# Transposing the first half batch from its float32 load tiles, moving the third to the DMA crossbar, and splitting the last output tile

## The chip, the cores and the metric

The kernel runs on one core of one Trainium2 chip. The metric is device time in microseconds (us) of one execution. Engines are called as the profile calls them: PE is the matrix engine, PEld its weight loads, DVE the vector engine, ACT the scalar engine, POOL the general engine, SP the engine that issues the DMA transfers.

## The reference

Sliding-window attention with four sink tokens feeds a gated feed-forward network:

```python
scores = scale * np.matmul(q, k.transpose(0, 1, 3, 2))          # B 4, H 8, S 768, D 64
keep = is_sink | in_window                                      # 4 sinks, window of 128
a = softmax(where(keep, scores, -1e9))
x = matmul(a, v).transpose(0, 2, 1, 3).reshape(3072, 512)
h = x @ w_in                                                    # 512 x 2048
g = h * (1.0 / (1.0 + np.exp(-beta * h)))
out = g @ w_out                                                 # 2048 x 512, float32
```

All inputs and the output are float32. Both kernels compute in bfloat16 after a cast.

## The kernel before

The work is cut into eight "half batches" of 384 tokens. Each has four units, a unit being a pair of heads. For a unit the kernel transposes q and k, computes scores, masks and exponentiates them, and multiplies by v. Then come the input projection (384-column matmuls) and the output projection (512-column matmuls) of the half batch. PE does all matmuls, so PE is the engine to keep busy.

The file is a small planner: it creates every instruction with a guess of its duration in ns, places the instructions on the engines by those guesses, and writes them out. From then on every engine has its own list, in a fixed order.

The half batches get their transposed q and k in one of two ways. `XB` says how many take the first way; the others take the second:

```python
# first way: cast to bf16, then six PE transposes per unit into one PSUM bank, one copy to SBUF
def T(u):
    ...
    for i, n in enumerate("qk"):
        for c in range(NK):
            add("pe", lambda e, i=i, n=n, c=c: nc.tensor.transpose(
                mp[:, i * HALF + c * 128:i * HALF + (c + 1) * 128],
                x16[n][hb % NX][:, c, 2 * hp:2 * hp + 2, :].rearrange("p h d -> p (h d)"), ident[:, :]),
                mm_ns(128), r=[(n + "16", hb % NX, hp, c), "ident"], x=[("B", bs[0])])
    any_of(copies(unitT(u).rearrange("p a (s j) -> p a s j", j=NK),
                  mp[:, 0:2 * HALF].rearrange("p (a j s) -> p a s j", a=2, j=NK), {"dve": 868, "act": 690}),
           w=qkey(u), x=[("B", bs[0])])

# second way: cast to bf16, then the DMA transposes q (or k) of the whole half batch
def XT(hb, i):
    ...
    add("sp", lambda e: e.dma_start_transpose(...), ...)
```

The window masks of the scores are `affine_select` instructions on POOL; the masks of the sinks may be on POOL or DVE. The output transposes of the first `XB` half batches are PE transposes as well; the later ones go through the crossbar. `mix` is the order in which early attention loads (`a`) and weight loads (`w`) are issued.

The softmax here doesn't subtract the row's maximum and nothing guards it: scores larger than these inputs give would overflow.

Of the kernel before, what the change touches and what calls it, by code (L numbers as in the profile page):

```python
# [22 lines left out]
PAR = {'AHEAD': 300,  # L23
 'BACKLOG': 3000,
 'KEEP': 300,
 'KEPT': 0,
 'MARGIN': 800,
 'M_AV': 200,
 'M_H': 0,
 'M_O': 0,  # L30
 'M_OT': 0,
 'M_SC': 1000,
 'M_SS': 2000,
 'M_T': 500,
 'XB': 3,
 'mix': 'wawawawwwawawwawwaaawwwawawaaaaa',
 'prio': ('SC', 'SS', 'OT', 'AV', 'T')}
# [7 lines left out]
class Graph:  # L45
# [8 lines left out]
    SLACK = 0  # L54
    LEAD = 1500
    COLD, WARM = 217, 150
# [68 lines left out]
    def place(self, o, at):  # L125
        o.at = at
        if o.dma:
# [11 lines left out]
            o.end = self.dma_free + 950  # L139
# [20 lines left out]
    def arrange(self):  # L160
# [37 lines left out]
        while todo_pe or pool:  # L198
# [14 lines left out]
            for o in pool:  # L213
                opts = []
                for e, (fn, ns) in o.alts.items():
                    t = max(self.free[e], ready(o, e))
                    if o.dma:
                        t = max(t, self.dma_free - self.LEAD)
                    opts.append((t + ns, t, e))
                _, t, e = min(opts)  # L220
                by_eng.setdefault(e, []).append((t, o))
# [161 lines left out]
def _program(nc, G, sb, ps, q, k, v, w_in, w_out, beta, out):  # L383
    NU = 2 * NPAIR
    NSTG, NX, NV, NT, NE, NON, NG, NTT, NOS, NKS, NWS = 2, 2, 3, 8, 4, 4, 3, 3, 3, 4, 6
    XB, PB = PAR.get('XB', 3), 2
    NK = NB // 2
    ident = sb("ident", (128, 128), BF16)
    ones = sb("ones", (128, 128), BF16)
    maskS = sb("maskS", (128, 2, 128), BF16)  # L390
# [32 lines left out]
    def unitT(u):  # L423
        return qkT_all[:, u // 4 % (NT // 4), :, :].rearrange("p a (h t) -> p a h t", h=4)[:, :, u % 4, :]

    def tokens(u, i, rows, t0, n):
        hb = u // 4
        if hb < XB:
            return unitT(u)[rows, i, t0:t0 + 128 * n].rearrange("p (s w) -> p s w", w=128)
        t = qkT_all[rows, hb % (NT // 4), i, :].rearrange("p (c h w) -> p c h w", h=4, w=128)  # L430
        return t[:, t0 // 128:t0 // 128 + n, u % 4, :]

    def qkey(u):
        return [("qkT", u % NT, i, c) for i in range(2) for c in range(NK)]

    def any_of(alts, r=(), w=(), x=()):

        return G.add(min(alts, key=lambda e: G.free[e] + alts[e][1]), None, 0, r, w, x, None, alts)
# [17 lines left out]
    def where(u):  # L456

        return u // 8, u // 4 % 2, u % 4
# [4 lines left out]
    def choose(n):  # L463

        if n == 4:
# [36 lines left out]
    def consts():  # L502
# [5 lines left out]
        for i, sg in ((0, -1), (1, 1)):  # L508
            add("gp", lambda e, i=i, sg=sg: e.affine_select(
                headm[:, i:i + 1], ones[:, 0:1], [[0, 1]], ALU.is_ge, 0.0, base=63 if i == 0 else -64,  # L510
                channel_multiplier=sg), 110, r=["ones"], w=["headm"] if i else ["headm0"])
        for i in range(NV):
# [12 lines left out]

        add("act", lambda e: e.activation(warm[:, :], ones[0:1, 0:1], AF.Exp, bias=0.0, scale=1.0), 1300,
# [17 lines left out]
    def load(hb, n, i):  # L544

        b, t0, z = hb // 2, hb % 2 * HALF, hb % NSTG
        if n != "v" and XB <= hb < XB + NSTG:
# [8 lines left out]
        elif hb >= XB:  # L556
# [30 lines left out]
    def cast(hb, n, i):  # L587
# [5 lines left out]
        elif hb < PB:  # L593
# [4 lines left out]
        elif hb >= XB:  # L598
# [5 lines left out]
        if hb < PB and n != "v":  # L604
# [13 lines left out]
    def T(u):  # L618

        G.begin()  # L620
        hb, hp = u // 4, u % 4
        bs = take(1)
        mp = P[:, bs[0], :].bitcast(BF16)
        for i, n in enumerate("qk"):
            for c in range(NK):
# [4 lines left out]
        any_of(copies(unitT(u).rearrange("p a (s j) -> p a s j", j=NK),  # L630
                      mp[:, 0:2 * HALF].rearrange("p (a j s) -> p a s j", a=2, j=NK), {"dve": 868, "act": 690}),
               w=qkey(u), x=[("B", bs[0])])
        sinks(u)
        give(bs)

    def sinks(u):
        hb, hp = u // 4, u % 4
        if hb % 2 == 0:
            ks = u % NKS
            kd = kS[ks][:, :].rearrange("p (a w) -> p a w", w=32)[:, 0:2, 0:NSINK]  # L640
            add("gp", lambda e: e.tensor_tensor(
                kd, tokens(u, 1, slice(0, 128), 0, 1)[:, :, 0:NSINK].to_broadcast([128, 2, NSINK]),
                headm[:, :].unsqueeze(2).to_broadcast([128, 2, NSINK]), ALU.mult), 200,
                r=[("kS", ks), ("qkT", u % NT, 1, 0), "headm0", "headm"], w=[("kSd", ks)])

    def XT(hb, i):
        n, s0 = "qk"[i], 4 * hb % NT
# [6 lines left out]
            w=[("qkT", s0 + j, i, c_) for j in range(4) for c_ in cs], dma=f"dx{n}{hb % 2}", queue=1540, ring=999, lag=1350)  # L654
# [7 lines left out]
    def slots(half):  # L662

        out_, i = {}, 0
        for j, grp in enumerate(GROUPS[half]):
# [5 lines left out]
    def SC(u):  # L671
        G.begin()
        b, half, hp = where(u)
        z = u % NE
        bs = take(4)
        for j, grp in enumerate(GROUPS[half]):

            jobs = {}
            for i, (kind, kb, qb) in enumerate(grp):
                jobs.setdefault(kb, []).append((qb, i))  # L680
            for kb, cols in jobs.items():
                cols.sort()
                own = u if kb >= NK * half else u - 4
# [3 lines left out]
                for hh in range(2):  # L687
# [4 lines left out]
                        dst, tokens(own, 1, rows, kc, 1)[:, 0, :], tokens(u, 0, rows, q0, nq),  # L692
                        start=True, stop=True), mm_ns(128 * nq) / 2 + 24,
                        r=qkey(u) + qkey(own), x=[("B", bs[2 * j + hh])])
        for j, grp in enumerate(GROUPS[half]):
            n, s0 = len(grp), slots(half)[grp[0]][1]
# [4 lines left out]
            for kind, sg in (("d", 1), ("p", -1)):  # L701
                at_ = [i for i, blk in enumerate(grp) if blk[0] == kind]
                if at_:
                    d = E[z][:, s0 + at_[0]:s0 + at_[-1] + 1, :, :].rearrange("p s h w -> p (s h) w")
                    add("gp", lambda e, d=d, sg=sg, at_=at_: e.affine_select(  # L705
                        d, d, [[0, 2 * len(at_)], [sg, 128]], ALU.is_ge, 0.0, base=min(sg, 0), channel_multiplier=-sg),
                        pool_ns(256 * len(at_), 2 * len(at_)), r=[("E", z, j)], w=[(kind, z, j)])
# [7 lines left out]
    def SS(u):  # L715

        G.begin()
        b, half, hp = where(u)
        z, ks = u % NE, (u - 4 * half) % NKS
        q0 = 0 if half else 256  # L720
        bs = take(1)
        add("pe", lambda e: e.matmul(  # L722
            P[:, bs[0], q0:HALF].rearrange("p (s w) -> p s w", w=128), kS[ks][:, :],
            tokens(u, 0, slice(0, 128), q0, (HALF - q0) // 128), start=True, stop=True), mm_ns(HALF - q0),
            r=[("kSd", ks)] + qkey(u), x=[("B", bs[0])])
        add("act", lambda e: e.activation(ES[z][:, q0:HALF], P[:, bs[0], q0:HALF], AF.Exp, bias=0.0, scale=SCALE),  # L726
            act_ns(HALF - q0), w=[("ES", z)], x=[("B", bs[0])])
        give(bs)

    def parts(half):  # L730

        sl = slots(half)
        return [[(blk[0], sl[blk][0], sl[blk][1], blk[1])
                 for blk in sorted(sl, key=lambda x: "spd".index(x[0])) if blk[2] == qb]
                for qb in range(NK * half, NK * half + NK)]

    def av_keys(u):
        z = u % NE
        ks = {(p[0], z, p[1]) for ps in parts(where(u)[1]) for p in ps}
        return sorted(ks) + [("v", u // 4 % NV, c) for c in range(NK)] + [("ES", z), ("vSd", u // 8 % 2, 1)]  # L740

    def AV(u):
        G.begin()
        b, half, hp = where(u)
        z, on = u % NE, u % NON
        bs = take(1)
        A = P[:, bs[0], :]
        for m, ps in enumerate(parts(half)):
            far = NK * half + m >= 2
            if far:  # L750
                c0 = 2 * m * (D + 1)
                add("pe", lambda e, m=m, c0=c0: e.matmul(  # L752
                    A[:, c0:c0 + 2 * (D + 1)], ES[z][:, m * 128:(m + 1) * 128],
# [3 lines left out]
            for hh in range(2):  # L757
                c0 = (2 * m + hh) * (D + 1)
                for n, (kind, j, i, kb) in enumerate(ps):
                    vz = (u if kb >= NK * half else u - 4) // 4 % NV  # L760
                    add("pe", lambda e, c0=c0, hh=hh, i=i, kb=kb, vz=vz, a=(n == 0 and not far), o=(n == len(ps) - 1):
                        e.matmul(A[:, c0:c0 + D + 1], E[z][:, i, hh, :], vaug[vz][:, kb % NK, 2 * hp + hh, :],  # L762
                                 start=a, stop=o, skip_group_check=True), 39,
                        r=[(kind, z, j), ("v", vz, kb % NK)], x=[("B", bs[0])])
        av = A[:, 0:2 * NK * (D + 1)].rearrange("p (a e) -> p a e", e=D + 1)
        add("dve", lambda e: e.reciprocal(rden[on][:, :].unsqueeze(2), av[:, :, D:D + 1]), 105,  # L766
# [326 lines left out]
```

## Time and profile before

| | before |
|---|---|
| median (range) of its runs | 230.72 us (230.68 to 231.6) |
| span of the profiled run | 228.6 us |
| PE busy | 96% |
| granted PE clock | 1.00 from the first record of it, at 6.1 us, to the last matmul |
| first input-projection matmul | 17.22 us |
| last v load issued | 143.0 us |

Two lines of the page give the busy time of each engine, in us, share of the span and instructions. After them comes the row of DMA busy tenths, with the span in 40 equal slices, then the line of the DMA queue that carries nearly everything (packets, MB, share of 16 engines' time), and the shares of the chain of work that ended last.

```profile
span 228.6 us, 4534 instructions
PE 218.7 (96%) x1756; PEld 121.5 (53%) x1756; DVE 137.1 (60%) x295; ACT 154.0 (67%) x276; POOL 72.6 (32%) x161
...
DMA  6999999999999999999999999621120311011112
...
q1 hardware_dynamic: 94112, 39.47, 75.8%
...
PE 79%; DVE 7%; DMA 7%; SPq 4%; ACT 2%; issue 1%; POOL 0%; POOLq 0%
```

PE is the limit, and 79% of the chain lies on it.

The timeline shows where the start ends and where the tail begins, as start, us, engine, line, operation, and in brackets the idle time before and what ended it. The waits view gives the only long wait of a projection, in us, times and longest.

```profile
17.22 1.73 PE L805 MATMUL P<-xT,w_in 128*128 128x384 bf16 x8
...
225.30 0.60 ACT L492 ACTIVATE osb<-P 128x512 f32<-128x512 f32 x1 [2.86 <-PE P L825]
```

```profile
PE P L805 <- DVE w_in L497: 2.0, 2, 1.1
```

### The profile page before, as it was taken

The numbers are of one execution on the slowest core, as the hardware profiler recorded it, in microseconds if no ns is written. First come the engines' busy times: TensorE is split into PE (matmuls) and PEld (weight loads), VectorE is DVE, ScalarE is ACT, GpSimd is POOL, SyncE is SP. The second block draws the span as 40 slices with busy tenths as digits, with TensorE's granted clock in tenths as the row PEclk, the third lists the DMA queues.
The fourth block names the chain that finished last, engine by engine and source line by source line (L and its number), as shares of the span: only waits on it lengthen the run. The fifth ranks groups of instructions, "written<-read, shape, count | busy, mean of one in ns | idle before, by whom it ended". The sixth has DMA issues, their size and how long they took to land.

```text
span 228.6 us, 4534 instructions
## 1 busy us (share of the span) xinstructions
PE 218.7 (96%) x1756; PEld 121.5 (53%) x1756; DVE 137.1 (60%) x295; ACT 154.0 (67%) x276; POOL 72.6 (32%) x161
## 2 busy tenths in 40 slices
PE   8987899989999999899999999999999999999994
PEld 5653454646555556455554554655556555555541
DVE  3697888467966787565766773655346433633310
ACT  2986897469867796676885847768778454744431
POOL 6590047523244861152241733204544000000000
PEclk9999999999999999999999999999999999999999
DMA  6999999999999999999999999621120311011112
GB/s 175 241 333 380 373 373 244 307 266 241 237 182 249 227 110 210 238 199 238 222 199 218 238 191 195 170 80 46 37 67 16 80 46 46 4 46 46 46 49 92
DMA packets 94133, 39.76 MB, mean 174 GB/s; under 512 B 80784, under 2 KB 86944, under 8 KB 94112
## 3 DMA queue, kind: packets, MB, share of 16 engines
q1 hardware_dynamic: 94112, 39.47, 75.8%
q8 instruction: 14, 0.23, 0.4%
q14 instruction: 7, 0.06, 0.1%
HBM read 27.27 MB, written 6.29 MB: 147 GB/s over the span
## 4 chain that ended last, share of the span: by engine, by line
PE 79%; DVE 7%; DMA 7%; SPq 4%; ACT 2%; issue 1%; POOL 0%; POOLq 0%
PE P L825 33%; PE P L805 30%; PE P L691 5%; DMA q_stage<-in_q_dram 4%; PE P L762 3%; DMA k_stage<-in_k_dram 3%; PE P L1019 2%; SPq L564 2%; PE P L626 2%; DVE onorm L768 2%; DVE g L812 2%; PE P L722 1%; PE P L752 1%; PE P L781 1%; DVE w_in L497 1%; ACT t L810 1%
## 5 line engine op out<-in xcount | busy, mean ns | idle before, releaser
L805 PE MATMUL P<-xT,w_in 128*128 128x384 bf16 x512 | 97.3, 326 | 2.4 <-DVE w_in L497 2.0
L810 ACT ACTIVATE t<-P,hbeta 128x384 f32<-128x384 f32 x128 | 73.7, 584 | 37.5 <-PE P L805 33.2
L825 PE MATMUL P<-w_out,g 128*128 128x512 bf16 x384 | 96.3, 379 | 0.9 <-DVE g L812 0.8
L812 DVE SCALAR_TENSOR_TENSOR g<-t,P 128x384 bf16<-128x384 f32 x128 | 69.0, 550 | 45.2 <-ACT t L810 43.4
L705 POOL TENSOR_SCALAR_AFFINE_SELECT E<-E 128x512 bf16<-128x512 bf16 (+1 forms) x112 | 57.2, 542 | 71.5 <-ACT E L699 71.0
L805 PEld LDWEIGHTS P<-xT,w_in 128*128 128x128 bf16 x512 | 47.6, 98 | 39.5 <-DVE w_in L497 3.2
L825 PEld LDWEIGHTS P<-w_out,g 128*128 128x128 bf16 x384 | 35.8, 98 | 37.1 <-DVE g L812 3.2
L699 ACT ACTIVATE E<-P 128x768 bf16<-128x768 f32 x64 | 45.2, 759 | 9.3 <-PE P L691 9.3
L492 ACT ACTIVATE osb<-P 128x512 f32<-128x512 f32 x22 | 13.1, 597 | 11.5 <-PE P L825 11.3
L762 PE MATMUL P<-vaug,E 128*128 128x65 bf16 x352 | 18.4, 193 | 0.5 <-DVE vaug L497 0.5
L768 DVE TENSOR_TENSOR onorm<-P,rden 128x384 bf16<-128x384 f32 x32 | 17.8, 556 | 1.0
L762 PEld LDWEIGHTS P<-vaug,E 128*128 128x128 bf16 x352 | 16.2, 97 | 3.1 <-DVE vaug L497 0.6
L497 DVE CAST q<-q_stage 128x512 bf16<-128x512 f32 (+1 forms) x21 | 10.9, 521 | 8.7 <-DMA q_stage<-in_q_dram 8.7
L691 PE MATMUL P<-qkT 64*128 64x128 bf16 (+1 forms) x256 | 15.8, 239 | 0.1
L691 PEld LDWEIGHTS P<-qkT 64*128 64x128 bf16 x256 | 8.7, 94 | 11.5 <-issue 6.6
L726 ACT ACTIVATE ES<-P 128x128 bf16<-128x128 f32 (+1 forms) x32 | 11.5, 393 | 3.0 <-PE P L722 3.0
L752 PE MATMUL P<-vS,ES 128*128 128x130 bf16 x64 | 12.6, 220 | 0.0
L711 DVE TENSOR_TENSOR E<-E,maskS 128x512 bf16<-128x512 bf16 x16 | 7.8, 488 | 6.7 <-ACT E L699 6.7
L497 DVE CAST vaug<-v_stage 128x512 bf16<-128x512 f32 x15 | 7.4, 493 | 5.3 <-DMA v_stage<-in_v_dram 5.2
L492 ACT ACTIVATE qkT<-P 128x768 bf16<-128x768 bf16 x10 | 8.1, 820 | 3.7 <-PE P L626 3.7
L497 DVE CAST k<-k_stage 128x512 bf16<-128x512 f32 (+1 forms) x19 | 8.7, 459 | 2.9 <-DMA k_stage<-in_k_dram 2.7
L766 DVE RECIPROCAL rden<-P 128x6 f32<-128x6 f32 x32 | 6.1, 190 | 6.9 <-PE P L762 6.8
(48 smaller groups left out, 98.3 us busy)
## 6 DMA issues: line engine op xcount, KB each, us to landing
v_stage<-in_v_dram SPq DMA_DIRECT2D x24, 256.0 KB, 5.2
out_dram<-osb SPq DMA_DIRECT2D x24, 256.0 KB, 2.8
q_stage<-in_q_dram SPq DMA_DIRECT2D x15, 256.0 KB, 5.1
k_stage<-in_k_dram SPq DMA_DIRECT2D x15, 256.0 KB, 5.1
wst<-in_moe_w_in_dram SPq DMA_DIRECT2D x5, 512.0 KB, 7.4
wst<-in_moe_w_out_dram SPq DMA_DIRECT2D x4, 512.0 KB, 9.3
g<-in_moe_w_out_dram SPq DMA_DIRECT2D x4, 512.0 KB, 9.0
q_stage<-in_q_dram SPq DMA_DIRECT2D x8, 192.0 KB, 5.1
```

What stands on the lines that cost most here:

```text
L492: return lambda e: e.activation(dst, src, AF.Copy, bias=0.0, scale=scale)
L497: return lambda e: e.tensor_copy(dst, src)
L691: add("pe", lambda e, dst=dst, own=own, kc=kc, rows=rows, q0=q0, nq=nq: e.matmul(dst, tokens(own, 1, rows, kc, 1)[:, 0, :], tokens(u, 0, r ...
L699: add("act", lambda e, src=src, dst_=dst_: e.activation(dst_, src, AF.Exp, bias=0.0, scale=SCALE), act_ns(256 * n), w=[(k_, z, j) for k_ i ...
L705: add("gp", lambda e, d=d, sg=sg, at_=at_: e.affine_select(d, d, [[0, 2 * len(at_)], [sg, 128]], ALU.is_ge, 0.0, base=min(sg, 0), channel_ ...
L752: add("pe", lambda e, m=m, c0=c0: e.matmul(A[:, c0:c0 + 2 * (D + 1)], ES[z][:, m * 128:(m + 1) * 128], vS[b % 2][:, 2 * hp:2 * hp + 2, :]. ...
L762: e.matmul(A[:, c0:c0 + D + 1], E[z][:, i, hh, :], vaug[vz][:, kb % NK, 2 * hp + hh, :], start=a, stop=o, skip_group_check=True), 39,
L768: add("dve", lambda e: e.tensor_tensor(onorm[:, on, :, :], av[:, :, 0:D], rden[on][:, :].unsqueeze(2).to_broadcast([128, 2 * NK, D]), ALU. ...
L805: add("pe", lambda e, c=c: e.matmul(hp, w_in16[:, c, m * 128:(m + 1) * 128], xT[:, T_, c, :], start=(c == 0), stop=(c == 3)), mm_ns(HALF), ...
L810: add("act", lambda e: e.activation(tt[ti][:, :], hp, AF.Tanh, bias=0.0, scale=hbeta[:, m:m + 1]), act_ns(HALF) + 93, r=["hbeta"], w=[("t" ...
L812: add("dve", lambda e: e.scalar_tensor_tensor(gt[T_ % NG][:, m, :], tt[ti][:, :], 1.0, hp, ALU.add, ALU.mult), dve_ns(HALF), r=[("t", ti)] ...
L825: add("pe", lambda e, m=m: e.matmul(P[:, bk, :], gt[T_ % NG][:, m, t * 128:(t + 1) * 128], w_out16[:, m, :], start=(m == 0), stop=(m == NM ...
```

## The change

The intent is to shorten the start, to take PE work out of the saturated middle, and to shorten the tail:

- `RAW`: half batch 0 is transposed straight from its float32 load tiles, without the casts, by float32 matmuls against a float32 identity. Two of them occupy the two column halves of the array.
- `XB` 3 to 2: half batch 2 takes the crossbar, for q, k and the output transposes.
- `PB` 2 to 1 and a new `mix`: half batch 1 is loaded as two whole tensors and not as eight head pairs, and weights come earlier.
- `MD`: DVE may do the window masks, by a multiplication, where only POOL could.
- `CUT`: the last output tile is computed as 384 and 128 columns, each copied and stored by itself.
- New priorities and margins of the planner.

```diff
 PAR = {
-'AHEAD': 300, 'KEEP': 300, 'KEPT': 0, 'M_AV': 200, 'M_O': 0, 'M_OT': 0, 'M_SC': 1000,
+'AHEAD': 600, 'KEEP': 500, 'KEPT': -1, 'M_AV': 1000, 'M_O': 200, 'M_OT': 1000, 'M_SC': 0,
+'MD': 8, 'PB': 1, 'RAW': 1, 'l0': [7, 3, 0, 6, 2, 10, 5, 1, 4, 8, 9],
-'XB': 3,
-'mix': 'wawawawwwawawwawwaaawwwawawaaaaa',
-'prio': ('SC', 'SS', 'OT', 'AV', 'T')}
+'XB': 2,
+'mix': 'wwwawwwaaawaaawawwwwaaaawawwaawa',
+'prio': ('OT', 'AV', 'SS', 'SC', 'T')}
...
-    SLACK = 0
+    SLACK = 200
+    BIAS, EARLY = 150, 45000          # copies cost ACT 150 ns more in the plan before 45 us
...
+    def TR(hb, hp):
+        bs = take(2)
+        for i, n in enumerate("qk"):
+            for c in range(NK):
+                for hh in range(2):
+                    add("pe", lambda e, i=i, n=n, c=c, hh=hh: e.matmul(
+                        P[64 * hh:64 * hh + 64, bs[i], c * 128:(c + 1) * 128],
+                        stg[n][hb % NSTG][:, 2 * hp + hh, c, :], identF[:, :], start=True, stop=True,
+                        tile_position=(0, 64 * hh)), 116, ...)
+        for i in range(2):
+            any_of(copies(headT(hb, hp)[:, i, :].rearrange("p (s j) -> p j s", j=NK),
+                          P[:, bs[i], 0:HALF].rearrange("p (j s) -> p j s", j=NK), {"dve": 465, "act": 380}), ...)
...
+                    if UNITS[u][0] < PAR.get('MD', 2):
+                        alts["dve"] = (lambda e, d=d, mk=mk: e.tensor_tensor(d, d, mk, ALU.mult), ...)
...
+    cut = PAR.get('CUT', 384)
+    if cut:
+        OS[-4:] = [OS[-4 + j] + ab for ab in ((0, cut), (cut, NOUT)) for j in range(4)]
```

The rest of the long diff generalises the planner for half batches in parts.

## The prediction

It was written before anything of the change had been built or run.

> What bounds the kernel now. The busy table gives PE 96% of 228.6 us at clock 1.0, but that overlaps pipelined matmuls and includes fillers, so I count pitches from the timeline: 162 ns per 384-column input-projection matmul (512, 83 us), 216 ns per 512-column output-projection matmul (384, 83 us), 0.44 us per score unit, about 0.48 per value unit, 56 ns per 128-column transpose. Estimate: 205 us of PE work. The other 24 us lie, by the same count per window, in the start before the first input-projection matmul at 17.2 us (5.7 us of real work, 47 fillers, 11.5 lost), in 17.2 to 33 us (about 4 lost: the waits show PE waiting 2.0 us for w_in casts on DVE, whose loads are interleaved with half batch 1 while the DMA engines are full), about 3.4 in 46 to 140 us, and 3.4 of tail after the last matmul at 225.3. After 33 us PE is the limit.
>
> What the change does.
> 1. Half batch 0: eight casts (DVE 0.4 us each, the first 1.43) leave the start; 24 bf16 transposes become 48 float32 matmuls. The Trainium skill (FP8 and Floating Point Precision) says true FP32 takes 4 passes; TensorEngine Tiling says tiles operate independently. Estimate: 128 columns x 4 at 2.4 GHz is 213 ns, two at a time, so 1.3 us per unit against 0.34 to 0.44. No run here shows it yet. It fills time that fillers fill today. The 0.8 us PSUM copy becomes two of about 0.5 that ACT and DVE can share. First scores move from 6.6 us to about 5.9; first input projection to about 15.5 us: 1.5 us gained.
> 2. Weights are loaded earlier in the mix (six of the first seven loads after half batch 0, not four); half batch 1 comes in two large loads plus v. The stalls in 17 to 33 us should shrink: 2 us gained, with the risk that half batch 1 comes late.
> 3. Half batch 2 by crossbar: 24 q/k transposes and 12 output transposes leave PE, 36 x 56 ns = 2.0 us in the saturated stage, fully critical; their copies leave ACT/DVE. It adds two q/k transposes (3.9 to 4.2 us to landing) and two output ones (3.7 us) on a DMA share near 1. Some comes back as late loads: 1.5 us net.
> 4. DVE may mask score blocks in place of POOL everywhere, and priorities are retuned: 0 to 1 us, uncertain in sign.
> 5. Last tile in 384 and 128 columns: the last copy falls from 0.60 to about 0.3 us and its transfer to 64 KB, against about 0.2 us more PE: 0.4 us net.
>
> Sum: about 6 us. Predicted 224.9 us, 80% range 221.5 to 228.5. Faster by over 2%: 0.65; within 2%: 0.33; slower: 0.02.
>
> What would show it. Right: no q/k cast of half batch 0; the first input-projection matmul before 16.2 us; fewer fillers; PE waits for w_in casts under 1 us; 12 crossbar q/k and 12 output transposes in place of 10 and 10; last matmul to end of span under 3.1 us; last matmul near 219 to 222 us. Wrong: the four float32 units last over 10 us; first projection no earlier.
>
> What would make it wrong: column tiles that do not overlap; a drain at each change of tiling; crossbar transfers that delay loads so that PE waits in 46 to 140 us; half batch 1 scores late, leaving PE with no work between input and output projection; or the start being bound by DMA arrival alone, so that nothing starts earlier.

## More of the kernel before

For the second way, and for v always, a row of a transfer is 256 bytes; for the first way it is 768 bytes:

```python
def load(hb, n, i):
    ...
    if n == "v":
        src = v[b, :, t0 + i * 128:t0 + (i + 1) * 128, :].rearrange("h p d -> p h d")      # 256-byte rows
    elif hb >= XB:
        src = {"q": q, "k": k}[n][b, :, t0 + i * 128:t0 + (i + 1) * 128, :].rearrange("h p d -> p h d")
    else:
        hs = slice(0, H) if i is None else slice(2 * i, 2 * i + 2)
        src = {"q": q, "k": k}[n][b, hs, t0:t0 + HALF, :].rearrange("h (p j) d -> p h (j d)", j=NK)  # 768
```

The windows view gives, for a stretch of time, its length and the busy us of PE, PEld, DVE, ACT and POOL (with instructions), the granted clock as a share, the DMA share and GB/s.

```profile
27.00:36.00 9.00, 9.00 (x66) 4.71 (x65) 7.95 (x16) 8.94 (x17) 3.19 (x5) 1.00 1.06 373
...
141.00:160.00 19.00, 19.00 (x151) 10.51 (x150) 11.07 (x25) 14.48 (x29) 4.95 (x12) 1.00 0.41 105
```

In both stretches PE never rests, and by the second the loads are nearly over (last v load issued at 143.0 us, DMA share 0.41).

## The result

The change was built as given and is correct. Ratios here and below are the mean time of one kernel's runs over that of the other's of the same rounds, with a 95% interval, so they are not quite the ratio of the medians quoted. Executions over 1.5% slower than the fastest of the same kernel are left out of the means.

| | before | after |
|---|---|---|
| median (range), same rounds | 230.80 us (230.68 to 231.6) | 234.22 us (233.63 to 234.91) |
| ratio | | 1.0142 (1.0106 to 1.0178) |
| span of the profiled run | 228.6 us | 232.5 us |
| first input-projection matmul | 17.22 us | 19.35 us |
| last v load issued | 143.0 us | 151.6 us |

The time went up by 1.4%. The prediction had said 224.9 us with a range up to 228.5. The same lines of the page, now of after:

```profile
span 232.5 us, 4595 instructions
PE 217.7 (94%) x1761; PEld 123.3 (53%) x1785; DVE 152.0 (65%) x343; ACT 147.5 (63%) x264; POOL 49.9 (21%) x115
...
DMA  6999999999999999999999999995151111011112
...
q1 hardware_dynamic: 103056, 40.65, 78.3%
...
PE 49%; DMA 26%; DVE 12%; SPq 7%; ACT 3%; issue 2%
```

The chain tells most: DMA goes from 7% to 26% of it, DVE from 7% to 12%, and PE from 79% to 49%. The page also gives the chain by line:

```profile
PE P L935 26%; PE P L913 19%; DMA v_stage<-in_v_dram 10%; DMA q_stage<-in_q_dram 5%; SPq L609 5%; DVE g L920 3%; DMA qkT<-q 3%; DMA wst<-in_moe_w_in_dram 2%; DVE onorm L871 2%; DMA k_stage<-in_k_dram 2%; PE P L864 2%; DMA xT<-onorm 2%; DMA qkT<-k 2%; PE P L784 2%; DVE w_in L536 1%
```

Most of the DMA share is loads, but 7% are landings of crossbar transposes (`qkT`, `xT`); the list of before has none. The DMA row stays at 9 for two more slices. (24 records of output-projection matmuls are missing from this trace, 376 of 400, so PE's busy sum is a little low.)

The windows of after:

```profile
27.00:36.00 9.00, 6.25 (x77) 3.71 (x75) 7.94 (x18) 7.25 (x14) 3.28 (x6) 1.00 1.02 266
...
141.00:160.00 19.00, 16.11 (x149) 8.70 (x151) 15.07 (x38) 13.77 (x28) 4.21 (x9) 1.00 1.08 210
```

PE has 2.75 us less of busy time in the first stretch and 2.89 us less in the second, and in the second the DMA share is 1.08 instead of 0.41: loads that were over by then are now under way.

To see where time is lost for good, I lined the two traces up by work. I counted the projection, score and value matmuls that both kernels do (199 us of PE work), and noted when each trace had done the same amount. The table gives after minus before, in us, at moments of before; the further rows are for the experiments. The profile of a control that runs the plan of before (f1 below) strays from before by up to 1.3 us, so differences of that size aren't read from single points.

| at, in before | 17 us | 27 | 31 | 36 | 50 | 61 | 82 | 140 | 156 | 225 |
|---|---|---|---|---|---|---|---|---|---|---|
| after | +2.1 | -0.7 | +4.4 | +4.8 | +2.6 | +1.5 | +1.5 | +1.1 | +4.8 | +4.6 |
| e2_copy_order | +1.5 | -1.4 | +3.6 | +3.9 | +1.7 | +0.6 | +0.5 | -0.1 | +2.1 | +1.7 |
| e4_weights_first | +2.4 | -0.5 | -0.2 | +5.5 | +3.6 | +3.2 | +5.3 | +6.8 | +8.8 | +8.3 |
| f1_control | +0.1 | 0.0 | +0.1 | +0.2 | +0.1 | +0.1 | +1.0 | -1.3 | -1.2 | -1.3 |
| f3_old_plus_xbar | 0.0 | 0.0 | 0.0 | 0.0 | -0.1 | -1.4 | +5.0 | +4.3 | +5.8 | +5.8 |
| f4_old_loads | +2.0 | +0.2 | +1.3 | +1.4 | +2.4 | +1.0 | +4.0 | +3.0 | +4.0 | +3.8 |
| g2_old_plus_f32 | +2.4 | +0.1 | +1.1 | +1.4 | +1.4 | +1.5 | +1.5 | +2.7 | +2.9 | +2.8 |
| h1_change_v_2k | +2.0 | -0.4 | +4.6 | +4.9 | +2.7 | +1.3 | +1.0 | -1.1 | +0.8 | +0.6 |

For after this reads as four events: the start is 2.1 us later; that is made good by 27 us; then 5.5 us are lost between 27 and 36 us; most of them are won back by 141 us; and 3.7 us are lost again between 141 and 160 us. The tail then gives back 0.6 us.

### Event 1: the start

These lines of after are PE from 3.7 us on, and the group of PSUM copies that follow the float32 transposes (busy us, mean ns of one, idle before).

```profile
3.73 1.52 PE L670 MATMUL P<-identF,q_stage 128*64 128x128 f32 x12
5.07 0.84 PE L670 MATMUL P<-identF,k_stage 128*64 128x128 f32 x12
5.74 0.82 PE L670 MATMUL P<-identF,q_stage 128*64 128x128 f32 x12
6.39 0.82 PE L670 MATMUL P<-identF,k_stage 128*64 128x128 f32 x12
...
7.30 0.45 PE L784 MATMUL P<-qkT 64*128 64x256 bf16 x8
```

```profile
L536 DVE CAST qkT<-P 128x384 bf16<-128x384 f32 x8 | 5.8, 803 | 5.4 <-PE P L670 5.3
```

A unit is 12 matmuls, which the trace records as 24. The Trainium skill (FP8 and Floating Point Precision, TensorE Precision Notes) says that true FP32 takes 4 passes through the array, and TensorEngine Tiling (Array Packing), Key Properties, says that tiles operate independently. The trace agrees with both: the records come in pairs that start 3 to 10 ns apart, a pair takes about 109 ns, and 12 pairs make the 1.3 us that the prediction had worked out. The second unit, from 5.74 to about 7.1 us, shows it. (By the pitches of before, 162 ns for 384 columns, four passes over 128 columns come to 216 ns, two matmuls at a time: the same estimate.) So the tiles do overlap. But two units stand before the first scores in PE's list, and the first unit takes 2.0 us: its pairs start about 213 ns apart until 5.1 us, twice the later distance. (The clock record of this trace starts only at 5.1 us, so the clock before that isn't known.) The first scores come at 7.30 us, where before had them at 6.59.

In before the same first copies looked like this:

```profile
L492 ACT ACTIVATE qkT<-P 128x768 bf16<-128x768 bf16 x10 | 8.1, 820 | 3.7 <-PE P L626 3.7
```

One copy of 0.82 us served q and k of a unit, on ACT. Now there are two of 0.80 us each, and all eight are on DVE, where the plan had reckoned with 0.465.

### Event 2: 27 to 36 us

The chain of waits of after (start, us, what) shows a weight block that comes late, and the SP timeline shows why:

```profile
28.52 5.71 DMA wst<-in_moe_w_in_dram
```

```profile
19.51 8.96 SPq L609 DMA_DIRECT2D v_stage<-in_v_dram  x3
28.52 1.41 SPq L620 DMA_DIRECT2D wst<-in_moe_w_in_dram  x2
```

The last two blocks of w_in are issued behind v of half batch 1, at 28.5 us. Half batch 1 itself, now in two loads of 768 KB, isn't there either: PE waits for the cast of its k.

```profile
27.71 0.33 PE L693 MATMUL P<-ident,q 128*128 128x128 bf16 x3
29.81 0.56 PE L693 MATMUL P<-ident,k 128*128 128x128 bf16 x3 [1.77 <-DVE k L536]
```

In before these microseconds were mostly filled with projections.

### Event 3: 36 to 141 us, and event 4: 141 to 160 us

Between 36 and 141 us after wins back 3.7 us. Of this 2.0 us would be, by count, the 36 transposes (24 of q and k, 12 of the output, 56 ns each) that half batch 2 no longer does on PE. The other 1.7 us I have not put down to anything single. In the fourth event the chain runs through a q load and a v load:

```profile
139.83 5.15 DMA q_stage<-in_q_dram
...
151.11 4.68 DMA v_stage<-in_v_dram
...
155.81 0.43 DVE vaug L536
```

In before the last v load was issued at 143.0 us, and the chain over this stretch is PE alone; its longest piece there is

```profile
143.92 2.60 PE P L805 x16
```

### The tail

From the last output copy to the end the prediction was right. This is the last copy of after, beside the 0.60 us of before:

```profile
229.74 0.28 ACT L531 ACTIVATE osb<-P 128x128 f32<-128x128 f32 x1 [0.40 <-PE P L935]
```

The last matmul lies 3.4 us before the end in before and 2.8 us in after.

### The profile page after: what moved, and what is told of

It reads as the page before. It is cut to its first block, busy times and chain, and to the rows that moved or that the text cites. A ratio compares the mean times of both kernels' runs of the same rounds, so it can differ in the third digit from the quotient of the medians.

```text
span 232.5 us, 4595 instructions
## 1 busy us (share of the span) xinstructions
PE 217.7 (94%) x1761; PEld 123.3 (53%) x1785; DVE 152.0 (65%) x343; ACT 147.5 (63%) x264; POOL 49.9 (21%) x115
## 4 chain that ended last, share of the span: by engine, by line
PE 49%; DMA 26%; DVE 12%; SPq 7%; ACT 3%; issue 2%
PE P L935 26%; PE P L913 19%; DMA v_stage<-in_v_dram 10%; DMA q_stage<-in_q_dram 5%; SPq L609 5%; DVE g L920 3%; DMA qkT<-q 3%; DMA wst<-in_moe_w_in_dram 2%; DVE onorm L871 2%; DMA k_stage<-in_k_dram 2%; PE P L864 2%; DMA xT<-onorm 2%; DMA qkT<-k 2%; PE P L784 2%; DVE w_in L536 1%
## 5 line engine op out<-in xcount | busy, mean ns | idle before, releaser
L935 PE MATMUL P<-w_out,g 128*128 128x512 bf16 (+2 forms) x376 | 92.2, 370 | 2.5 <-DVE rden L869 0.9
L935 PEld LDWEIGHTS P<-w_out,g 128*128 128x128 bf16 x400 | 36.8, 98 | 34.5 <-DVE g L920 1.3
L799 POOL TENSOR_SCALAR_AFFINE_SELECT E<-E 128x256 bf16<-128x256 bf16 (+1 forms) x63 | 34.3, 552 | 73.0 <-ACT E L793 71.7
L804 DVE TENSOR_TENSOR E<-E,maskT 128x256 bf16<-128x256 bf16 (+1 forms) x49 | 18.6, 399 | 5.1 <-ACT E L793 4.8
L531 ACT ACTIVATE osb<-P 128x512 f32<-128x512 f32 (+2 forms) x21 | 12.1, 577 | 9.2 <-PE P L935 9.2
L536 DVE CAST vaug<-v_stage 128x512 bf16<-128x512 f32 x18 | 8.0, 447 | 6.7 <-DMA v_stage<-in_v_dram 6.5
L536 DVE CAST qkT<-P 128x384 bf16<-128x384 f32 x8 | 5.8, 803 | 5.4 <-PE P L670 5.3
L821 PE MATMUL P<-qkT,kS 128*128 128x128 bf16 (+1 forms) x32 | 8.2, 277 | 0.8 <-DVE g L920 0.5
L536 DVE CAST q<-q_stage 128x512 bf16<-128x512 f32 x13 | 5.9, 456 | 4.3 <-DMA q_stage<-in_q_dram 4.2
```

Source lines behind the costliest of these rows:

```text
L536: return lambda e: e.tensor_copy(dst, src)
L799: alts = {"gp": (lambda e, d=d, sg=sg, at_=at_: e.affine_select(d, d, [[0, 2 * len(at_)], [sg, 128]], ALU.is_ge, 0.0, base=min(sg, 0), cha ...
L804: alts["dve"] = (lambda e, d=d, mk=mk: e.tensor_tensor(d, d, mk, ALU.mult), 70 + 256 * len(at_) / 1.9)
L935: add("pe", lambda e, m=m: e.matmul(P[:, bk, a:b], gt[hb % NG][:, m, t * 128:(t + 1) * 128], w_out16[:, m, a:b], start=(m == 0), stop=(m = ...
```

## The experiments

Two theories stood against each other.

- **Own costs.** The new parts cost more than was thought, wherever they stand: the float32 path at the start, the crossbar transfers as DMA time.
- **Order.** The parts are worth what was predicted, but the load order and the retuned plan put casts, loads and matmuls in a worse order.

Eighteen kernels were run, each timed against before. As the changed program holds all switches, an experiment is mostly a change of settings. "Control" means the changed program with every switch set back. The experiments called old_plus put one part of the change into the control; those that undo a part start from the whole change.

### Does the control stand for before, and what is the tail worth?

f1_control:

```diff
-RAW=1, XB=2, PB=1, MD=8, CUT=384, new mix, prio, margins, SLACK=200, BIAS=150
+RAW=0, XB=3, PB=2, MD=0, CUT=0,   old mix, prio, margins, SLACK=0,   BIAS=0
```

> The changed kernel's code with every switch set back: bf16 transposes, half batch 2 on PE, no cut, the old load order, priorities and margins, masks on POOL. A control: within 1% of before (229 to 232.5), first input-projection matmul 17 to 17.6 us, last v load issued before 146 us. If it is far off, what remains of the new code (three more constants on POOL, another cost table, another choice of banks) has an effect of its own and the single changes below must be read against this run, not against before.

Measured: 229.31 us, ratio 1.0009 (0.9992 to 1.0025), first projection at 17.32 us. The control stands for before.

f2_old_plus_cut, the control with the last tile in two parts:

```diff
-CUT=0
+CUT=384
```

> The control with only the last tile cut into 384 and 128 columns. Tail after the last matmul 2.9 us instead of 3.4 and at most 0.3 us more PE: 0.2 to 0.5 us faster than the control.

Measured: 229.07 us, ratio 0.9991 (0.9977 to 1.0006). In the profile the tail after the last matmul is shorter, and the medians differ by 0.24 us, but the interval still holds 1. It is the best correct version found, by a margin that isn't a result.

### The float32 transposes

g2_old_plus_f32, the control with this part alone:

```diff
-RAW=0
+RAW=1
```

> The control with only the float32 transposes of half batch 0, strided PSUM copies as in the change. If the float32 path makes the start late: first input-projection matmul at 18.3 to 19.5 us against 17.3, and 0.5 to 2 us slower than the control. If it is only the change's steering of copies away from ACT: no later than 17.6 us, since the control has no such steering.

Measured: 233.29 us, ratio 1.0134 (1.0106 to 1.0163), first projection at 19.89 us. So this part alone brings the late start (+2.4 us in the table) and is 1.3% slower, though no load and no mask was changed. The eight copies were on ACT here, at 824 ns each: ACT is no faster than DVE at them.

The new copy writes every third element of the bfloat16 destination. The same copy can be written in the order of the destination, so that the jumps are on the PSUM side. g3_old_plus_f32_cp does this in the control, e2_copy_order in the whole change; the values are the same, and the plan is too, since the planner's guesses aren't touched:

```diff
-headT(hb, hp)[:, i, :].rearrange("p (s j) -> p j s", j=NK), P[...].rearrange("p (j s) -> p j s", j=NK)
+headT(hb, hp)[:, i, :].rearrange("p (s j) -> p s j", j=NK), P[...].rearrange("p (j s) -> p s j", j=NK)
```

> As g2 with the copies walking SBUF contiguously. The copy takes 0.56 us on DVE, as in e2, and the start gains 0.5 to 1 us on g2; the kernel is within 0.7 us of the control.

> The changed kernel with the float32 path kept, only the order in which its PSUM copies walk is turned round: SBUF written contiguously, PSUM read with a stride, as the bf16 copy does. If DVE's 0.80 us comes from the strided 2-byte writes, one copy falls to about 0.45 us and the first input-projection matmul comes 1 to 2.5 us earlier than 19.35. If it comes from reading float32 PSUM, the copy stays at 0.80 and nothing moves. If the float32 matmuls themselves (1.3 us per unit) were the limit, the copy may fall but the first input projection stays within 0.5 us of 19.35.

Measured: g3 232.82 us, ratio 1.0112 (1.0067 to 1.0157), first projection at 18.97 us; e2 231.82 us, ratio 1.0082 (1.0007 to 1.0158), first projection at 18.68 us. The copies fell to 496 ns on ACT in g3 and 558 ns on DVE in e2, as the view of the tile in e2 shows (durations in ns as minimum, median, maximum, then first and last start):

```profile
L536 DVE CAST qkT<-P x8: 545/558/558, 5.3 to 11.9; 128x384 bf16<-128x384 f32 x8
```

The first projection came 0.7 to 0.9 us earlier. The stride of the write is a real cost of the change, and mended it brings the start from +2.1 to +1.5 us, not to a gain. That is less than e2's expectation of 1 to 2.5 us, and g3, 1.1% slower than before, missed its own of 0.7 us from the control. On the whole time the intervals overlap with those of the unmended kernels.

e1_no_f32 undoes the part within the whole change:

```diff
-RAW=1
+RAW=0
```

> The changed kernel with half batch 0 transposed again by bf16 casts and bf16 transposes, nothing else undone. Theory A (the start is late because the eight float32 PSUM copies, 0.80 us each, all stand on DVE in front of masks and casts): first input-projection matmul moves from 19.35 us back to about 17.2, and the kernel takes about 232.5 us, so 1 to 2 us less than the 234.2 of the change. Rival (the start is late for the new load order or the new engine choice for masks, not for the float32 path): first input-projection matmul stays above 18.8 us.

Measured: 238.81 us over four executions, of which one, 241.07 us, was slow; ratio of the fast ones 1.0340 (1.0251 to 1.0428), first projection at 18.46 us. The start is earlier than in after, but well short of the 17.2 us of theory A, and the kernel is 2% slower than the whole change. The settings came with the float32 path, and with the casts put back the plan fits worse. I read the plan as the reason, and have no run that shows it alone; the trace also has two stretches of 3.4 us (from 16.8 and from 27.1 us) in which the granted clock was 0.50. This run taught me to trust additions to the control more than subtractions from a tuned whole.

### The masks on DVE

h4_dve_masks_cut is the control with the cut, and with DVE allowed to mask in half batches 0 and 1; i1_change_pool_masks is the change without that choice; i2_pool_masks_copy is i1 with the copy order of e2 as well.

```diff
# h4, from the control with the cut    # i1 and i2, from the change
-MD=0                                  -MD=8
+MD=2                                  +MD=0
```

> The control with the cut and with DVE allowed to mask the score blocks of half batches 0 and 1. If waiting for POOL masks is part of the start, the first input-projection matmul comes before 17 us and the kernel takes 228 to 229 us; if DVE is the fuller engine at the start, it comes later than 17.5 us and the time is 229 to 231.

> The changed kernel with all score masks back on POOL. If DVE is the full engine at the start, the first input-projection matmul comes at 18.3 to 19 us instead of 19.35. Over the whole run: within 3 us of 234.2, as each change of one switch makes another plan (e1, e3 and e4 were 2.5 to 5 us slower).

> As i1, with the contiguous copies of e2. If the copies and the masks on DVE are all of the late start, the first input-projection matmul comes at 17.2 to 18 us; if float32 matmuls or their count of copies cost more, it stays above 18 us (g3, without masks on DVE, was at 18.97). Time under e2's 231.8 if the start carries through to the end.

Measured: h4 231.96 us, ratio 1.0064 (1.0014 to 1.0113), first projection at 18.00 us; i1 232.77 us, ratio 1.0078 (1.0016 to 1.0140), at 19.21 us; i2 232.59 us, ratio 1.0083 (1.0048 to 1.0118), at 19.57 us. On the old plan the DVE masks delay the first projection by 0.7 us and cost some time. DVE already makes the casts at the start. But i2, with both suspects at the start removed, still starts at 19.57 us. So neither the stride nor the masks explain the late start of the whole change. What is left is the float32 matmuls with their two copies per unit (g3, on the old plan, starts at 18.97 us) and the order of the new plan (e1, without float32, starts at 18.46 us). Which share each has stays open. The masks on POOL may be worth up to 0.6% in the change; the intervals of i1 and of after overlap.

### The crossbar for half batch 2

f3_old_plus_xbar, the control with this part alone:

```diff
-XB=3
+XB=2
```

> The control with only half batch 2 moved to the crossbar. Theory B (DMA engine time bounds the loads): DMA packet time rises by 7 to 10 us, the last v load is issued at 148 to 153 us instead of 143, PE work falls by 2.0 us, and the time does not fall: same as the control or up to 4 us slower. Rival (crossbar is worth its 2 us of PE and the late stall has another cause): 1 to 2 us faster than the control.

Measured: 235.39 us, ratio 1.0276 (1.0253 to 1.0298), last v load at 153.2 us against 141.0 in the control. The table shows both sides. By 61 us the kernel has gained 1.4 us, which fits the transposes saved. Then it loses 6.4 us by 82 us. The chain shows the place:

```profile
72.16 1.60 SPq L898
...
75.05 5.60 DMA v_stage<-in_v_dram
...
80.68 0.53 DVE vaug L538
```

A crossbar transpose of outputs (line 898) is issued ahead of v of half batch 3, on the same SP list, so v is issued at 73.8 to 75 us and lands at 80.65 us. In the control these three v loads went out from 66.46 us. The first line is the SP list of the control, the two after it that of f3:

```profile
66.46 2.22 SPq L611 DMA_DIRECT2D v_stage<-in_v_dram  x3
```

```profile
72.02 1.74 SPq L898 DMA_TRANSPOSE xT<-onorm  x1
73.81 2.18 SPq L611 DMA_DIRECT2D v_stage<-in_v_dram  x3
```

So here the order of the SP list is at work, the rival that g1's expectation names, and not only a slower transfer. PE starves, and then there is a second price. Two windows of f3, PE only (busy, clock, DMA share, GB/s), and the projections that start in them; last, the second window in the control, with all engines:

```profile
80.00:82.40 2.40, 1.78 (x26) 0.50 1.25 169
82.40:85.00 2.60, 2.60 (x13) 0.50 1.37 222
```

```profile
82.39 3.94 PE L915 MATMUL P<-xT,w_in 128*128 128x384 bf16 x12
```

```profile
82.40:85.00 2.60, 2.60 (x18) 1.57 (x17) 2.56 (x7) 2.60 (x8) 2.60 (x6) 1.00 1.76 175
```

The granted clock is 0.50, and in windows of 1 us it stays there from before 80 to 86 us; the projections start 320 ns apart instead of 163. The Trainium skill (TensorE: Matmul & The Clock Gate, What's actually happening) describes two states, half clock when idle and full clock after sustained work. The trace agrees on the two levels, 0.50 and 1.00; PE was not idle before this fall, though (last section). Some 6 us at half clock are at most about 3 us of lost work, an estimate from these windows. So f3 overstates what the crossbar costs in the whole change, where the clock is 1.00 in every window that I read. Two of the four executions of f3 had a mean clock of 0.993 and not 0.985, about half as long at half clock, and took as long (235.25 and 235.42 us), so the clock isn't the whole of the 2.8%.

What does the DMA pay? The queue lines of the control and of f3:

```profile
q1 hardware_dynamic: 94112, 39.47, 74.5%
```

```profile
q1 hardware_dynamic: 103008, 40.65, 76.4%
```

The packet time, the share times the span, goes from 169.5 to 179.1 us per engine: 9.6 us more, for about 8,900 more packets. They are of two kinds: the q and k of half batch 2 now come in 256-byte rows, 6,144 packets in place of 2,048 of 768 bytes, and the four added transposes bring 4,608 packets of 256 bytes. The figure has a large spread, though: before (173.4 us), f1 (169.5), g3 (174.1) and g2 (177.5) moved the same 94,112 packets. Over the runs with v in 256-byte rows, the eight with half batch 2 on the crossbar had 175.6 to 184.7 us, the eight with it on PE, g1 and h3 aside, 166.4 to 177.5; the means are 9 us apart. So the 9 us stand as a mean, but a few us between two single runs say little. g1_rows_256 pays for the first kind alone: the control, with half batch 2 loaded in 256-byte rows but still transposed on PE.

```diff
-return "block" if hb in PARTS else "pair" if hb < PB else "whole" if hb < XB else "xbar"
+return "block" if hb in PARTS or hb == 2 else "pair" if hb < PB else "whole" if hb < XB else "xbar"
```

> The control with half batch 2 loaded in the 256-byte rows that the crossbar needs, in the same order as in f3, but transposed on PE: the row size without the crossbar. Against f1 (229.3 us, 169.5 us of DMA packet time, last v load issued at 141.0) and f3 (235.4, 179.1, 153.2). If the crossbar transposes cost the DMA time: packet time at most 3 us above f1 and time within 1.5 us of f1. If the small rows do: packet time 5 us or more above f1 and time over 232.5. Rival to both (f3 is slow since the transposes block the queue in order, not for DMA time): time within 1.5 us of f1 although packet time rises.

Measured: 234.76 us, ratio 1.0198 (1.0148 to 1.0247). The packet time of all queues rises from 170.7 us in f1 to 175.5 us, half of what f3 adds. That is between the two thresholds of the expectation, and within the spread just given, so that smaller rows are half the DMA cost of the crossbar way isn't shown. Here too a loss falls on one wait behind an output transpose: v is issued at 102.56 us, lands 5.59 us later, and PE runs short of work.

```profile
100.67 1.22 SPq L901
...
102.56 5.59 DMA v_stage<-in_v_dram
```

```profile
105.00:110.00 5.00, 3.48 (x47) 0.94 1.24 156
110.00:115.00 5.00, 5.00 (x44) 0.72 1.19 193
```

As the windows (PE only) show, g1 too pays at half clock, for 3.4 us from 109.4 us. It isn't a clean split of the time, because the transposes and copies are then grouped by blocks of tokens, and the planner placed other things around them.

The other direction is h3_hb3_pe_cut, the control with the cut and one half batch more on PE:

```diff
-XB=3, CUT=0
+XB=4, CUT=384
```

> The control with the cut and with one half batch more on PE (half batches 0 to 3; the crossbar has 16 transposes instead of 20). Theory B run backwards: packet time 7 to 10 us less than f1, last v load issued before 137 us, PE 2.0 us more work. Time 229 to 231.5: the DMA time saved buys little where PE is the limit. Rival (moving a half batch mostly disturbs the plan): over 233 us.

Measured: 231.79 us, ratio 1.0065 (1.0024 to 1.0106). The last v load is issued at 121.6 us, 19 us earlier than in the control, and the share of the queue falls:

```profile
q1 hardware_dynamic: 85360, 38.29, 68.1%
```

The time is still 0.7% longer than before. PE now has 36 transposes more, 2.0 us by count; that these are the loss is my reading, the trace wasn't followed. With two half batches on PE (f3) or with four (h3) the kernel is slower than with the three of before.

e3_hb2_pe takes the crossbar out of the whole change:

```diff
-XB=2
+XB=3
```

> The changed kernel with half batch 2 transposed on PE again and loaded in 768-byte rows. Theory B (the loads are bounded by DMA engine time; half batch 2 by crossbar adds about 9 us of it, so the last half batches arrive late and PE stalls for 3.7 us between 141 and 160 us): last v load issued before 146 us, stall in 140 to 162 us under 1.5 us, PE 2 us more work, time 231.5 to 233.5. Rival (crossbar saves PE 2 us and costs nothing; the late stall comes from the new priorities and in-order queues): stall stays above 3 us and the time rises by about 2 us to 236.

Measured: 238.71 us, ratio 1.0361 (1.0290 to 1.0432), slower than the change itself. The late wait was gone and the last v load was issued at 142.8 us, as I had expected. But PE was 9 to 10 us behind before that; between 33 and 46 us it was busy 9.79 of 13.00 us, with the chain on DVE and ACT. My reading, not shown, is that the load order string holds other loads when half batch 2 comes as whole tensors. Like e1 it says little about the part, and much about subtracting from a tuned plan.

### The order of loads

f4_old_loads puts the old load order back into the change; e4_weights_first moves the last w_in blocks ahead; g4_no_xbar_old_loads has the old order and no crossbar for half batch 2.

```diff
# f4                        # g4                       # e4
-PB=1, new mix              -XB=2, PB=1, new mix       -mix='wwwawwwaaawaaawawwwwaaaawawwaawa'
+PB=2, old mix              +XB=3, PB=2, old mix       +mix='wwwawwwwwaaaaaawwwwaawwaawwaawaa'
```

> The changed kernel with the old loads of half batch 1 (eight pairs of heads instead of two whole tensors) and the old mix of weights and activations; all else as changed. Theory C' (the stall of PE in 27 to 36 us is due to the load order: v of half batch 1, at 225 GB/s, before the last weights): the delay against before at 14 to 20 us of common work falls from 4.4 to under 2 us. By the end, theory B says the last v load is still issued near 150 us, so at most 2 us are kept: 231.5 to 234.

> The changed kernel with the last two input-projection weight blocks loaded before the v of half batch 1 instead of after it; all else kept. Theory C (PE stands still in 27.7 to 36 us because those two blocks are issued only at 28.5 us): the delay of 4.4 us against before at 35 us falls to about 1 us. Whether the end moves: if DMA time bounds the end (theory B), most is given back by 160 us and the time falls by less than 1.5 us; if PE alone bounds, the time falls by about 3 us to 231.

> The change without its crossbar half batch and with the old loads: float32 transposes, masks on DVE, new priorities and the cut remain. If crossbar and load order together make the loss after the start, what is left is the start: 230 to 232 us, no stall over 1 us between 27 and 36 nor between 140 and 160 us, last v load before 146 us. If the new priorities and the masks on DVE cost time of their own: over 233 us.

Measured: f4 233.51 us, ratio 1.0178 (1.0148 to 1.0208); e4 237.62 us, ratio 1.0312 (1.0254 to 1.0371); g4 233.62 us, ratio 1.0135 (1.0090 to 1.0180). The early wait does come from the load order: in f4 the lag at 36 us is 1.4 us in place of 4.8, and in e4 it is -0.2 us at 31 us. But neither kernel is faster for it. f4 loses the time at 74 to 86 us, where v of the next half batch is late. e4 loses it by 36 us (+5.5): k of half batch 1 now lands at 30.0 us in place of 28.8, and the chain from 28 to 43 us lies mostly on DVE and ACT. In these two kernels moving one load ahead pushed another back, and the wait changed its place.

g4 is the run that speaks against a single cause. It has neither the crossbar half batch nor the new loads, its last v load is issued at 141.2 us and its packet time is 171.7 us, both near the control's 141.0 and 169.5, and yet it is as slow as the whole change. By its own expectation (over 233 us) the float32 transposes, the masks on DVE and the priorities cost time of their own; g2 gives 1.3% for the first alone. So the crossbar is enough for a loss (f3), but the loss doesn't need it, and the parts don't add up.

### Is DMA time the common cause?

If it is, freeing DMA time without touching anything else must bring the change back to the level of before. h1_change_v_2k and h2_control_v_2k read v in 2048-byte rows, with as many bytes and as many transfers, in the same order of the SP list. The values land in wrong places, so the results are wrong (relative error 1.39 against the reference); I take it that time doesn't depend on the values, which no run tests.

```diff
-src = v[b, :, t0 + i * 128:t0 + (i + 1) * 128, :].rearrange("h p d -> p h d")
-dst, keys, ns = stg[n][z][:, i, :, :], [i], 1185
+src = v[b, 2 * i:2 * i + 2, :, :].rearrange("h s d -> (h s d)")[0:65536].rearrange("(p x) -> p x", x=512)
+dst, keys, ns = stg[n][z][:, i, :, :].rearrange("p h d -> p (h d)"), [i], 1185
```

> The changed kernel, wrong on purpose: every v load fetches the same bytes per partition from a contiguous piece of v, so 2048-byte rows in place of 256-byte rows. All engines keep their order of instructions. Theory B (DMA time of small rows and crossbar transposes delays the loads): DMA packet time falls by over 10 us, the last v load is issued before 146 us, the stalls at 27 to 36 and 141 to 160 us shrink by 3 us or more together, and the kernel falls from 234.2 to 229 to 231.5 us. Rival (the stalls come from the order of work on queues and engines): over 233 us although packet time falls.

> The control of f1 with the same wrong v loads. If before is bounded by PE after 46 us, as predicted, it gains at most 1.5 us on 229.3; if DMA time bounds it too, 2 us or more. Either way it should gain less than the changed kernel gains in h1.

The queue lines of h1 and of h2:

```profile
q1 hardware_dynamic: 81552, 40.65, 75.1%
```

```profile
q1 hardware_dynamic: 72608, 39.47, 68.8%
```

Measured: h1 229.22 us, ratio 0.9945 (0.9886 to 1.0005); h2 229.09 us, ratio 0.9944 (0.9905 to 0.9983). The packet time falls by 10 us in the change (from 181.9 to 171.7) and by 13 us in the control. The control gains 0.6%; the change gains about 2%, and the two meet, to within the 0.6% of h1's interval. So with DMA time to spare the change costs nothing that these intervals can show, and without it 1.4% (the 1.4% was measured in another session, against its own runs of before). Two of the expectations for h1 failed: the last v load is issued at 147.4 us and not before 146, and the two stalls together shrink by about 2 us and not by 3. Of the 4 us that the table shows won by the end, half are won between 36 and 140 us. Nor does the run separate the DMA engines from the issuing: the SP instructions that issue v last 26.6 us in all in after and 17.9 in h1 (30.0 in the control, 15.0 in h2). So "DMA time" here means the whole way of a load, issue and packets. The late wait shrinks: this is h1 in the stretch where PE of after was busy 16.11 us.

```profile
141.00:160.00 19.00, 17.62 (x159) 9.76 (x162) 14.21 (x36) 14.87 (x29) 5.85 (x11) 1.00 0.80 169
```

The early wait doesn't shrink, +4.6 us at 31 us as in after, though the last two w_in blocks were issued at 21.9 us in place of 28.5 and had landed by 31.4 us. Their casts stand behind other DVE instructions and were run at 34.2 us and later. So this part belongs to the order theory. It costs little in the end: h1 is only 0.6 us behind before at 225 us. The cleaner half of the answer is the DMA half.

## Why the prediction was wrong

Several signs that the prediction named held (fillers 47 to 24, waits of PE for w_in casts 2.0 to 0.2 us, tail 2.8 us, 12 and 12 crossbar transposes), and the time rose all the same. What failed were steps 3, 1 and 2, each by its sign; which of them is the largest part of the 1.4% isn't shown, as g4 has the same loss without step 3 and step 2.

**Step 3, the crossbar, had the wrong sign.** The prediction said "2.0 us in the saturated stage, fully critical" and "Some comes back as late loads: 1.5 us net". The 2.0 us are likely real: f3 was 1.4 us ahead by 61 us, and after regained more than that. What failed is the term for what comes back. I had looked at the time from issue to landing of each transpose (about 4 us; in after such landings make 7% of the chain), and not at the sum: packet time per engine rises by 9.6 us in f3, on DMA engines that were busy at 9 tenths for 143 us. The later loads came later, the last v load by 8.6 us (143.0 to 151.6), and PE then lost 3.7 us between 141 and 160 us. Packet time isn't all of this delay: in h1, with 171.7 us of it, less than before has, the last v load still goes out at 147.4 us, and in f3 v stood behind a transpose in the SP list. Alone, on the old plan, the part costs 2.8%, with the stretch at half clock in it. "What would make it wrong" named exactly this, but the sum gave it half a microsecond.

**Step 1, the start, had the wrong sign.** Predicted was the first projection at about 15.5 us; it came at 19.35 us. The float32 matmuls took the 1.3 us that I had estimated in the second unit, so that term stood but for the first unit. Failed were two others. The copies were put at "two of about 0.5 that ACT and DVE can share": they took 0.80 us each, against 0.50 to 0.56 in the order of the destination, and they stood on one engine. The Trainium skill (TensorEngine Tiling (Array Packing), PSUM Bottleneck) says to use both engines for them, and the plan didn't. And I treated the 1.3 us as filling time that fillers fill: yet two units stand before the first scores in PE's list, and the first of them took 2.0 us. The first scores came at 7.30 us and not at 5.9. The copy order gives back 0.7 to 0.9 us, and g2 shows that the part brings the late start on the old plan as well. The rest of the late start in the whole change is left open (i2).

**Step 2, the early waits, had the wrong sign.** Instead of shrinking by 2 us they grew to nearly 5 us at 36 us. I had counted weights among the first seven loads and not where the last two w_in blocks stood, behind v of half batch 1. The prediction named the risk "that half batch 1 comes late", and it was this, with w_in as well. That the order is the cause is shown by f4, which puts back `PB` and `mix` together; in e4 the wait is gone at 31 us and back at 36. That mending it alone brings nothing is shown by the same two.

**Step 4, masks and priorities**, left open in sign, came out negative where it could be tested: h4 costs 0.1 to 1.1%.

**Step 5, the tail, was right** in mechanism. The last copy fell from 0.60 to 0.28 us and the tail by 0.6 us in the profile; the time fell by about 0.2 us, half the 0.4 us predicted, within the noise.

The deeper error is in how the sum was made. Each step was costed mostly on PE and the gains were added up. The crossbar step, and the order of the loads, spend DMA time, of which the page showed hardly any to be left, and h1 shows the loss gone once the way of the v loads is made shorter. That this is DMA engine time, and not the issuing or the order of the SP list, stays open.

## What to carry to other kernels

When the DMA row stands at 9 tenths for most of a kernel, cost a change by the packet time that it adds to the queue (bytes, and the length of the rows), even if no transfer is on the chain now. Taking work from the busiest engine onto one that is nearly full can cost more than it saves: here 2.0 us of PE work saved, and 2.8% lost (f3). Compare packet times of several runs, as the same packets took 169 to 178 us here. If you want to know what one part of a tuned change is worth, add it alone to the old kernel as well as taking it out of the new one: taking it out also breaks the tuning around it. And before moving a load forward, ask which load moves back.

## What the Trainium skill lacked or had wrong

- DMA: Bandwidth & Descriptors, Why small descriptors are slow (HBM only), gives 11 cycles for a 256-byte descriptor, 27% of them overhead. In the control the trace has 23 ns as the mean time of a 256-byte packet (median 18; those of the crossbar transposes are among them) and 94 ns of a 2048-byte one (median 85), 1.7 times (medians) to twice (means) as long per byte, so more than the overhead stated in that section.
- No page that I read gives the price of a strided bfloat16 write in a PSUM copy. For 128x384 float32 to bfloat16 with every third element written it was 803 ns on DVE and 824 ns on ACT; in the order of the destination 558 and 496 ns.
- TensorE: Matmul & The Clock Gate, What's actually happening, has the clock fall after an idle window of about 3.4 us. In f3 it fell to 0.50 at 79.3 us with PE busy 2.35 of 4.00 us between 76 and 80 us, and it came back at 86 us, after more than 3.4 us of nearly unbroken work; in after it stayed at 1.00 with PE busy 6.25 of 9.00 us. How sparse the work may get before it falls isn't stated. The stretches at half clock in the traces last 3.4 us (g1, e1) or 6.8 us (f3), one or two of the stated windows.
- TensorEngine Tiling (Array Packing), Key Properties, says that a change of tiling mode drains the array. No run here isolates that cost. That pairs of float32 column tiles overlap, 109 ns a pair, is confirmed and is stated there without a time.
